# A new build-time order for a fused attention and expert kernel: counting DMA issues, the shared port of VectorE and GpSimd, idle PSUM banks and filler transposes

## The chip, the cores and the metric

The kernel runs on one core of one Trainium2 chip. The metric is the device time of one execution in microseconds, taken as the median of several executions. Each experiment was timed against the kernel before on the same chip in the same rounds. e1 to e4 ran on one chip and e5 to e12 on another. The kernel before took 1820.07 us on the first, and 1820.44 and 1820.51 us on the second, so a comparison of e1 with a later run can be off by about half a microsecond.

## The reference, cut to what matters

```python
# attention without softmax: 8 batches, 8 heads, 576 rows, 64 columns
kv  = einsum('bhsd,bhse->bhde', k, v)
out = einsum('bhsd,bhde->bhse', q, kv)
x   = out / sqrt(mean(out*out, -1) + 1e-6) * g_norm      # RMS norm
x   = x.transpose(0, 2, 1, 3).reshape(4608, 512)
# four experts, all of them applied to every row
p   = domain_probs / (domain_probs.sum(-1) + 1e-9)
for e in range(4):
    h    = maximum(x @ w1[e], 0)           # 512 -> 1024
    out += p[:, e:e+1] * (h @ w2[e])       # 1024 -> 512
```

Everything is float32. The 4608 rows are worked on as nine chunks of 512 rows, so there are 36 pairs of an up product (`w1`) and a down product (`w2`). In the attention, a "pair" is a pair of heads: a batch is worked on as four of them.

## The kernel before

Both products use a two-level scheme of block products in which seven products replace eight. It pays with additions: sums of blocks of `w1`, of `w2` and of `x` must exist before TensorE can multiply, and sums of results must be made after. VectorE and GpSimd make these sums; ScalarE copies and squares.

The order of all instructions is decided in Python when the kernel is built. Each operation has a key (how early it is wanted), an estimated cost on each engine that could do it, the buffers it reads and the buffers it writes. A simulation then runs through time and gives each free engine the ready operation with the smallest key:

```python
class Plan:
    CROSS, SAME = 0.3, 0.06
    REACH = {"PE": 0.7, "DVE": 0.9, "ACT": 0.9, "POOL": 0.9, "SP": 1.0}
    ...
    def layout(self, slots):
        ...
        while left:
            ...
            for eng in todo:                       # each engine that is free at time t
                for op in pending:                 # by key
                    when = ready(op, eng)          # inputs made, a buffer free
                    ...
                    if eng == "SP":                # a DMA issue
                        busy[eng] = t + op.cost[eng]
                        bus = max(bus, t + 1.5) + op.kb / 215.0
                        op.end = bus + 0.5
```

The parts that the change touches are the PSUM banks (the buffers into which TensorE writes its results; the kernel uses eight), the loads of the first attention batch, the weight sums, and the stores of the `x` sums:

```python
BANKS = {"ub": 4, "db": 2, "ab": 2}        # up products, down products, attention
SPC = {"SP": 0.08}                         # planned cost of one DMA issue
...
def combine(key, cost, out_, a, b, op, reads, writes):     # one sum, VectorE or GpSimd
    plan.add(key, cost, lambda eng: adder(eng).tensor_tensor(...), reads=reads, writes=writes)
...
def weights_1(e, key, step):
    ... # four loads of 512 KB, then the sums follow the loads at once
    form(key + 4 * step, 5, 21, 4, ALU.add)                # 1024 wide
    ...
    k2 = key + (8 + j) * step                              # 256 wide, four per outer block
...
def x_forms(c, key, step):                 # sums of x, then stores of 192 KB and 256 KB
    ...
attention(0, -2.0, 1.3, 0.1)               # keys: smaller is earlier
weights_1(0, -0.9, 0.02)
x_views = {0: x_forms(0, -0.2, 0.02)}
weights_2(0, 0.0, 0.02)
```

## Time and profile before

| quantity | before |
|---|---|
| time, median of 3 runs | 1820.47 us (1819.86 to 1820.76) |
| TensorE busy | 1784.6 us, 98% of the span of 1818.3 us |
| VectorE busy | 1126.2 us, 62% |
| GpSimd busy | 475.1 us, 26% |
| first up product starts | 41.76 us |
| first down product starts | 86.45 us |

TensorE is full but for the first 100 us. In a line of the windows below, the first two numbers are the stretch and its length; then come the busy microseconds (with the number of instructions) of TensorE, its weight loads, VectorE, ScalarE and GpSimd; then TensorE's granted clock, the share of the DMA engines and their GB/s. The prediction shows these rows up to 40 us. The next two of the kernel before are:

```profile
40.00:50.00 10.00, 9.98 (x63) 9.37 (x64) 9.33 (x17) 4.72 (x11) 9.84 (x17) 0.72 1.10 236
50.00:60.00 10.00, 6.88 (x70) 6.31 (x70) 9.90 (x15) 3.13 (x10) 6.50 (x5) 0.96 0.82 268
```

TensorE has gaps or a low clock here while VectorE is full (9.33 and 9.90 of 10). Below, "warm" means TensorE at full clock and "cold" at half of it. From the groups of the page come the two that make the large sums (line, engine, operation, shapes, count, then busy us and mean ns of one, then idle time before them and what ended it):

```profile
L276 DVE TENSOR_TENSOR big<-big,big 128x1024 f32<-128x1024 f32 x343 | 474.8, 1384 | 55.1 <-ACT big L680 33.2
...
L276 POOL TENSOR_TENSOR big<-big,big 128x1024 f32<-128x1024 f32 x85 | 209.0, 2462 | 1116.7 <-DVE big L276 976.1
```

VectorE's mean of 1384 ns is above the 1.22 us that one takes alone: some of them stood behind a GpSimd operation.

### The profile page before, as it was taken

The numbers are of one execution on the slowest core, as the hardware profiler recorded it, in microseconds if no ns is written. First come the engines' busy times: TensorE is split into PE (matmuls) and PEld (weight loads), VectorE is DVE, ScalarE is ACT, GpSimd is POOL, SyncE is SP. The second block draws the span as 40 slices with busy tenths as digits, with TensorE's granted clock in tenths as the row PEclk, the third lists the DMA queues.
The fourth block names the chain that finished last, engine by engine and source line by source line (L and its number), as shares of the span: only waits on it lengthen the run. The fifth ranks groups of instructions, "written<-read, shape, count | busy, mean of one in ns | idle before, by whom it ended". The sixth has DMA issues, their size and how long they took to land.

```text
span 1818.3 us, 32290 instructions
## 1 busy us (share of the span) xinstructions
PE 1784.6 (98%) x12496; PEld 1660.7 (91%) x12496; DVE 1126.2 (62%) x1841; ACT 608.4 (33%) x1345; POOL 475.1 (26%) x426
## 2 busy tenths in 40 slices
PE   5899999999999999999999999999999999999999
PEld 4889999999999999999999999999999999999997
DVE  6866665666676555555666555555566655556554
ACT  2544344443333333333333333333333333333331
POOL 4565554646364000000145000000036100000001
PEclk7999999999999999999999999999999999999999
DMA  9764444424433333334434333333434333343321
GB/s 231 179 167 141 128 139 126 135 95 139 132 109 119 117 114 115 114 113 134 136 130 152 118 118 118 118 118 121 147 127 163 117 115 117 118 118 116 115 74 35
DMA packets 192089, 228.96 MB, mean 126 GB/s; under 512 B 54464, under 2 KB 123328, under 8 KB 191936
## 3 DMA queue, kind: packets, MB, share of 16 engines
q1 hardware_dynamic: 191936, 226.89, 40.9%
q8 instruction: 99, 1.62, 0.4%
q14 instruction: 54, 0.44, 0.1%
HBM read 160.18 MB, written 66.65 MB: 125 GB/s over the span
## 4 chain that ended last, share of the span: by engine, by line
PE 94%; DVE 2%; SPq 2%; DMA 1%; issue 1%; POOL 0%; ACT 0%; DVEq 0%; ACTq 0%
PE ub L697 42%; PE db L831 29%; PE ab L831 18%; SPq L282 1%; PE ab L504 1%; PE ab L486 1%; DVE big L276 1%; PE ab L514 1%; PE ab L471 1%; DVE small L276 0%; DMA big<-in_moe_w_dram 0%; DMA small<-in_q_dram 0%; PE ab L553 0%; DVE big L718 0%; POOL big L276 0%
## 5 line engine op out<-in xcount | busy, mean ns | idle before, releaser
L831 PE MATMUL db<-big,big 128*128 128x256 f32 x2520 | 596.3, 380 | 1.7 <-DVE big L276 1.3
L697 PEld LDWEIGHTS ub<-small,big 128*128 128x128 f32 x3816 | 498.4, 192 | 23.4 <-issue 1.4
L697 PE MATMUL ub<-small,big 128*128 128x128 f32 x3816 | 513.5, 276 | 0.4 <-DVE big L718 0.4
L276 DVE TENSOR_TENSOR big<-big,big 128x1024 f32<-128x1024 f32 x343 | 474.8, 1384 | 55.1 <-ACT big L680 33.2
L831 PEld LDWEIGHTS db<-big,big 128*128 128x128 f32 x2520 | 455.2, 190 | 51.7 <-DVE big L276 1.5
L276 POOL TENSOR_TENSOR big<-big,big 128x1024 f32<-128x1024 f32 x85 | 209.0, 2462 | 1116.7 <-DVE big L276 976.1
L710 ACT ACTIVATE snap<-ub 128x256 f32<-128x256 f32 x756 | 285.5, 383 | 556.7 <-PE ub L697 500.8
L718 DVE TENSOR_TENSOR big<-ub,snap 128x256 f32<-128x256 f32 x756 | 307.0, 421 | 216.7 <-PE ub L697 163.1
L697 PE MATMUL ub<-small,w1y 128*128 128x128 f32 x2916 | 384.9, 276 | 2.2 <-DVE big L718 2.1
L697 PEld LDWEIGHTS ub<-small,w1y 128*128 128x128 f32 x2916 | 360.5, 192 | 7.9 <-DVE big L718 2.9
L831 PE MATMUL ab<-big,big 128*128 128x256 f32 x1512 | 357.4, 380 | 1.7 <-DVE small L788 1.7
L831 PEld LDWEIGHTS ab<-big,big 128*128 128x128 f32 x1512 | 273.2, 190 | 32.0 <-DVE small L788 2.1
L710 ACT ACTIVATE big<-ub 128x256 f32<-128x256 f32 x252 | 96.7, 384 | 414.6 <-PE ub L697 410.1
L788 DVE SCALAR_TENSOR_TENSOR small<-db,p_all,small 128x256 f32<-128x256 f32 x243 | 116.9, 481 | 139.8 <-PE db L831 139.2
L788 DVE SCALAR_TENSOR_TENSOR small<-ab,p_all,small 128x256 f32<-128x256 f32 x189 | 91.1, 482 | 177.3 <-PE ab L831 177.3
L680 ACT ACTIVATE big<-big 128x1024 f32<-128x1024 f32 x144 | 152.0, 1055 | 107.8 <-DVE big L276 104.8
L784 DVE TENSOR_SCALAR small<-db,p_all 128x256 f32<-128x256 f32 x72 | 34.6, 481 | 54.1 <-PE db L831 54.1
L425 POOL TENSOR_TENSOR rt<-ss,mhalf 128x8 f32<-128x8 f32 (+1 forms) x40 | 65.7, 1643 | 3.3
L421 POOL TENSOR_SCALAR ss<-ss 128x8 f32<-128x8 f32 (+1 forms) x40 | 15.6, 391 | 101.0 <-DVE ss L416 99.6
L416 DVE TENSOR_REDUCE ss<-small 128x8 f32<-128x512 f32 (+1 forms) x40 | 27.1, 678 | 22.3 <-ACT small L411 22.3
L504 PE MATMUL ab<-kvbd,small 128*128 128x128 f32 x256 | 38.3, 298 | 1.6 <-ACT kvbd L494 1.6
L432 DVE TENSOR_TENSOR small<-ab,rt 128x512 f32<-128x512 f32 (+1 forms) x40 | 27.4, 686 | 17.3 <-POOL rt L425 17.1
(63 smaller groups left out, 664.0 us busy)
## 6 DMA issues: line engine op xcount, KB each, us to landing
small<-x SPq DMA_DIRECT2D x189, 256.0 KB, 3.5
small<-x SPq DMA_DIRECT2D x189, 192.0 KB, 2.9
o<-small SPq DMA_DIRECT2D x108, 256.0 KB, 2.0
small<-o SPq DMA_DIRECT2D x108, 256.0 KB, 2.8
big<-in_moe_w_dram SPq DMA_DIRECT2D x32, 512.0 KB, 5.0
x<-small SPq DMA_DIRECT2D x63, 256.0 KB, 3.1
small<-in_q_dram SPq DMA_DIRECT2D x72, 128.0 KB, 3.9
kv<-in_k_dram SPq DMA_DIRECT2D x32, 288.0 KB, 3.5
```

The lines of the kernel that those rows point to most:

```text
L276: lambda eng: adder(eng).tensor_tensor(out=out_(), in0=a(), in1=b(), op=op),
L416: lambda eng: nc.vector.reduce_sum(out=ss.ap[0:n, :], in_=rows(sq), axis=AX.X),
L425: nc.gpsimd.tensor_tensor(out=rt.ap[0:n, :], in0=ss.ap[0:n, :], in1=mhalf[0:n, :], op=ALU.pow)
L432: lambda eng: nc.vector.tensor_tensor(out=rows(x), in0=rows(raw), in1=rt.ap[0:n, :].unsqueeze(2).to_broadcast([n, H, D]), op=ALU.mult,),
L504: nc.tensor.matmul(raw.ap[:, rs], lhsT=qT.ap[:, rs], rhs=kb.ap[:])
L680: lambda eng: nc.scalar.activation(out=b.ap[:], in_=b.ap[:], func=ACT.Relu),
L697: nc.tensor.matmul(ps.ap[:, u * P:(u + 1) * P], lhsT=w1f[e][m][mm][1]()[:, u * P:(u + 1) * P], rhs=views[m][mm][1](), start=(mm in (1, 2, ...
L710: lambda eng: nc.scalar.activation(out=where(), in_=ps.ap[:, 0:HN], func=ACT.Copy),
L718: lambda eng: nc.vector.tensor_tensor(out=block(whole, a, t), in0=src.ap[:, 0:HN], in1=add_.ap[:], op=ALU.add),
L784: nc.vector.tensor_scalar_mul(out=acc[i].ap[:, cols], in0=ps.ap[:, 0:HN], scalar1=prob)
L788: nc.vector.scalar_tensor_tensor(out=acc[i].ap[:, cols], in0=ps.ap[:, 0:HN], scalar=prob, in1=acc[i].ap[:, cols], op0=ALU.mult, op1=ALU.add,)
L831: nc.tensor.matmul(ps.ap[:, 0:HN], lhsT=four(h[m])[:, kt // 2, t, kt % 2, :], rhs=w2f[e][m].ap[:, kt * HN:(kt + 1) * HN], start=(m in (1, ...
```

## The change

Its intent is that the build-time order should be closer to what the chip does, and that the start should be shorter. It has six parts:

1. The order counts a DMA issue as 0.55 us in place of 0.08, and allows eight transfers in flight.
2. Two sums on VectorE and GpSimd never overlap in the plan (`port=True`).
3. Batch 0 of the attention uses the PSUM banks of the up and down products, which are idle then. TensorE gets filler transposes where the plan has it idle before the first up product.
4. All `q`, `k` and `v` of batch 0 are loaded first, two of the four pairs into big buffers. The up weights come next and the down weights later.
5. The weight sums have keys close to their use (`need`), so they come after the attention.
6. The `x` sums are made and stored in fewer and larger pieces.

Smaller parts came with these: the corner of a weight buffer that a sum writes over is tracked apart from the rest of the buffer, a block of an up product may start only after the last product of the block two before it, and only DMA issues must leave some buffers free.

```diff
-    CROSS, SAME = 0.3, 0.06
+    CROSS, SAME, LANES = 0.3, 0.06, 8
...
+            if eng == "SP":
+                when = max(when, lanes[0])
+            if op.port:
+                when = max(when, port)
             return when
...
+                if eng == "PE" and busy[eng] <= t and 1.6 <= t and front < idle_until:
+                    ...                      # two transposes of the identity into a free bank
-    BANKS = {"ub": 4, "db": 2, "ab": 2}
+    BANKS = {"u1": 2, "u2": 2, "db": 2, "ab": 2}
-    SPC = {"SP": 0.08}
+    SPC = {"SP": 0.55}
...
-            reads=reads, writes=writes,
+            reads=reads, writes=writes, port=True,
...
-        form(key + 4 * step, 5, 21, 4, ALU.add)
+        form(need + 0.25, 5, 21, 4, ALU.add)
...
-            kt, vt, qt = Buf("kv", f"k{n}"), Buf("kv", f"v{n}"), Buf("small", f"q{n}")
+            kind = "kv" if b or hp < 2 else "big"
+            kt, vt, qt = Buf(kind, f"k{n}"), Buf(kind, f"v{n}"), Buf("small", f"q{n}")
+            want = at(hp) - 0.25 if b else key - 1 + 0.1 * hp
...
-            bank = Buf("ab", f"kv{n}")
+            bank = Buf("ab" if b else "u1", f"kv{n}")
...                                          # x sums: one 256-wide and two 128-wide, not four 128-wide
...                                          # stores of 256 and 512 KB, not 192 and 256 KB
-    weights_1(0, -0.9, 0.02)
-    x_views = {0: x_forms(0, -0.2, 0.02)}
-    weights_2(0, 0.0, 0.02)
+    weights_1(0, -2.5, 0.02, -0.35)
+    x_views = {0: x_forms(0, -0.3)}
+    weights_2(0, 0.25, 0.02)
...
-                weights_1(e + 1, s + 0.0, 0.12)
+                weights_1(e + 1, s + 0.0, 0.12, s + 0.3)
...
-    order = plan.layout(slots)
+    order = plan.layout(slots, idle, ("u1", "u2", "db"), 0.0)
```

## The prediction

> **What bounds the kernel now.** I read the page first, then the table of windows, then the timelines of TensorE and VectorE over the first 160 us, then the chain of what ended last.
>
> ```profile
> PE 1784.6 (98%) x12496; PEld 1660.7 (91%) x12496; DVE 1126.2 (62%) x1841; ACT 608.4 (33%) x1345; POOL 475.1 (26%) x426
> ...
> PE   5899999999999999999999999999999999999999
> ```
>
> TensorE is busy all the time except in the first two slices of 45 us. The chain says how long a steady chunk takes; its rows have start, duration, engine, line:
>
> ```profile
> 198.06 1.78 PE ub L697 x16
> ...
> 257.86 1.78 PE ub L697 x16
> ...
> 688.75 3.12 PE ub L697 x28
> 734.81 3.12 PE ub L697 x28
> ```
>
> The same row of two neighbouring chunks is 46.06 us apart in the later experts and 59.80 us in the first one, where a batch of attention (59.80 - 46.06 = about 13.7 us) is mixed in. 36 chunks and 8 batches make 36 x 46.06 + 8 x 13.7 = 1768 us of TensorE work at full clock. The last product ends near 1813.8, and 4.5 us of merge and store follow. So 1813.8 - 1768 = 46 us are lost, and the windows show where (start:end, length, then busy time of each engine, clock):
>
> ```profile
> 0.00:10.00 10.00, 2.57 (x28) 2.11 (x29) 1.21 (x9) 1.88 (x2) 0.69 (x6) 1.00 0.69 153
> 10.00:20.00 10.00, 8.15 (x54) 6.81 (x52) 2.40 (x4) 3.78 (x9) 3.40 (x4) 1.00 1.13 317
> 20.00:30.00 10.00, 8.21 (x72) 7.09 (x72) 9.47 (x13) 2.93 (x8) 5.12 (x3) 0.58 1.18 246
> 30.00:40.00 10.00, 1.48 (x6) 0.79 (x6) 8.99 (x19) 1.28 (x2) 7.92 (x9) 0.50 0.80 207
> ...
> 600.00:900.00 300.00, 300.00 (x2003) 281.05 (x2002) 175.44 (x292) 93.05 (x206) 14.18 (x6) 1.00 0.39 123
> ```
>
> In 600 to 900 TensorE has no gap at all. Between 150 and 1800 the windows lack about 4 us of TensorE busy time in total, most of it where one expert's weights give way to the next. So some 42 of the 46 us are lost before 150 us. From 20 to 60 us VectorE is the full engine and TensorE waits for it:
>
> ```profile
> 28.28 2.08 PE L504 MATMUL ab<-kvbd,small 128*128 128x128 f32 x8 [0.55 <-ACT kvbd L494]
> 34.70 1.11 PE L514 MATMUL ab<-ident,small 128*128 128x128 f32 x4 [4.33 <-DVE small L432]
> 40.02 1.09 PE L514 MATMUL ab<-ident,small 128*128 128x128 f32 x4 [4.21 <-DVE small L432]
> 40.90 1.06 PE L471 MATMUL ab<-ident,small 128*128 128x128 f32 x4
> 41.76 1.91 PE L697 MATMUL ub<-big,big 128*128 128x128 f32 x8
> ...
> 108.03 1.05 PE L504 MATMUL ab<-kvbd,small 128*128 128x128 f32 x8
> ```
>
> The first up product starts at 41.76. By then 12.7 us of useful work are done (batch 0 of the attention, counted with the warm durations), so 29 us are lost. By the first down product at 86.45 the same count gives 42 us. The rest up to 157 us adds a little. The x8 group of L504 takes about 2.0 us early and 1.05 us later: TensorE runs at half clock then, though the page grants 1.00 in the first windows.
>
> **What the Trainium skill says.** (1) "TensorE: Matmul & The Clock Gate", Part 1, states that the array starts at half rate and reaches full rate after a busy window of about 3.4 us. The 2.08 against 1.05 us agrees with two rates. (2) The same page, Part 4, says that transposes do not count as TensorE busy time in the same way. This matters, since the change fills gaps with transposes; the trace before doesn't decide it. (3) "SBUF — State Buffer", section "SBUF: two separate sides", describes the port pair of VectorE and GpSimd as an exclusive lock, whose loser waits out the whole instruction. The trace agrees exactly:
>
> ```profile
> 20.36 4.84 POOL L276 TENSOR_TENSOR big<-big,big 128x1024 f32<-128x1024 f32 x2
> ...
> 21.04 1.95 DVE L276 TENSOR_TENSOR w1y<-big 128x256 f32<-128x256 f32 x1
> ...
> 22.91 3.37 DVE L276 TENSOR_TENSOR big<-big,big 128x1024 f32<-128x1024 f32 x1
> ```
>
> The two GpSimd operations take 2.42 us each and end at 22.78 and 25.20. VectorE's 256-wide operation, 0.42 us when alone, ends just after the first; its 1024-wide one, 1.22 us alone, ends about 1.1 us after the second. (4) "DMA: Bandwidth & Descriptors", section "Bandwidth", advises large transfers. Here the average DMA share after 150 us is 0.4, so the size of the stores can't matter much.
>
> **The change, part by part.** *x sums in larger pieces.* The order of issues shrinks from 961 to 745 rows. Bytes grow: per reload 7 x 512 KB instead of 7 x 448 KB, 0.45 MB more per 46 us, or 10 GB/s on about 120. No wait of TensorE after 150 us is put down to a DMA, so this is worth 0. Three additions per form become one 256-wide and two 128-wide (0.335 + 2 x 0.205 us by the spacing in VectorE's timeline, against 4 x 0.205): 7 x 0.08 = 0.5 us per chunk of an engine that has slack once the start is over.
>
> *Loads.* All q, k, v of batch 0 now come first, then expert 0's up weights, then batch 1, then the down weights. The four pairs are 3.33 MB. Before, 1.53 MB had moved by 10 us and 317 GB/s flowed after it, so the fourth pair lands near 10 + 1.8/0.317 = 15.7 us, and the up weights (2.1 MB) near 22. Before, the third pair's product started at 22.1 and the fourth's at 26.2. From the key-value product (8.52) to the last transposes (16.99) one pair took 8.5 us, so the fourth could reach its transposes near 24.2.
>
> *Fillers.* The changed order has 130 extra 128x128 transposes of the identity, 118 of them ahead of the first up product. A group of four takes about 0.44 us warm, so the 118 take 13.0 us warm and 26 us at half clock. They stand in TensorE's queue with the 12.3 us of real work: from 1.5 us on, 25.3 us of it, so the first up product can't start before about 27. With the first microseconds cold and a few waits on top I put it at 30. That is 11 to 12 us earlier than 41.76.
>
> *The VectorE order.* Attention now comes ahead of the weight sums on VectorE: the reductions of all four pairs stand before the first weight sum, so the 4.2 and 4.3 us waits go. But the weight sums are put off, not removed. Counting VectorE's rows in the new order with the durations above (1.13 us per 1024-wide, 0.6 per 512 and per reduction, 0.335 per 256, 0.2 per 128) gives about 41 us from the fourth pair's multiplication to the 21st sum of an up block (seven blocks' worth). The old order gives about 42 us for the like stretch and took 65 us for it (18.2 to 84). If the new order starts at 24.5 and loses 8 to 15 us to the port and to waits, in place of 24, it gets there at 74 to 81 us. TensorE will then have done 51.7 us of useful work by my count of its order, so 22 to 29 us are lost, against 42 to 43 before. That is 14 to 21 us won.
>
> *Rest.* Experts 2 to 4, the tail and the 4 us between experts stay: the products are the same, and in the new order two up blocks still run alternately with one down product in every five. The sum: 1820.5 less about 19 is **1801 us**.
>
> **The rivals.** *VectorE takes the place of the old wait.* If the fillers and earlier loads only bring TensorE sooner to a VectorE that is full anyway, the gain is 8 us or less, 1812. For: 9.47, 8.99, then 9.33 and 9.90 us busy out of each 10 between 20 and 60. Against: part of that was blocked time. *Cold fillers.* If transposes don't raise the clock, 118 of them cost 26 us, the first up product starts near 45, and the change is worth nothing or costs up to 8 us: 1820 to 1828. For: the skill's sentence. Against: real products stand among them and raised the clock before; the groups at 18.88 and 20.23 take 0.66 us, not 1.09. *New steady waits.* The up products get two pairs of banks instead of a pool of four, and port-exclusive planning may misplace sums. At 0.3 us a chunk this would eat 11 us: 1812. Against: about 3 us of other products stand between two writes of one bank, twice the copy and sum they wait for. *All goes well*: VectorE is never blocked and arrives at 68, then 1791.
>
> **Range and chances.** The best case loses 30 - 12.7 = 17 us before the first up product even with nothing after it, so more than 36 us cannot be won and faster by over 2% is nearly excluded. Slower by over 2% needs 1 us lost per chunk, which the even order speaks against. I take 1788 to 1815 with 1801 in the middle: faster 0.02, same 0.95, slower 0.03.
>
> **What would show it.** Right: first up product between 27 and 33; transposes of the last pair without 4 us waits; the first down product near 65 to 75; VectorE still above 9 of 10 between 30 and 60; GpSimd's and VectorE's 1024-wide operations no longer stretched; a steady chunk of 46.06 us; stalls between experts unchanged. Wrong: four transposes at 1.09 us up to 40 us (cold fillers); gaps of TensorE between 150 and 1800 over 10 us in total; a chunk over 46.3 us; or a first down product after 80.

## The result, and the profile after

| quantity | before | after |
|---|---|---|
| time, median (range) of 4 runs each | 1820.16 us (1819.74 to 1820.76) | 1806.80 us (1805.55 to 1807.96) |
| span of the profiled run | 1818.3 us | 1803.8 us |
| first up product starts | 41.76 us | 28.93 us |
| first down product starts | 86.45 us | 67.92 us |
| TensorE idle after 150 us (of the stretches to 1700 us) | 3.63 us | 1.25 us |

The ratio is 0.9926, with a 95% interval of 0.9909 to 0.9943: 13.4 us won. A ratio is the mean time of one kernel's runs over that of the other's in the same rounds, so it is not quite the ratio of the medians quoted. The idle time of a stretch is its length less TensorE's busy time.

These are the lines of the page after that answer to those of before:

```profile
PE 1788.7 (99%) x12626; PEld 1667.9 (92%) x12626; DVE 1010.0 (56%) x1757; ACT 614.3 (34%) x1345; POOL 582.0 (32%) x447
...
PE   8999999999999999999999999999999999999998
...
L304 POOL TENSOR_TENSOR big<-big,big 128x1024 f32<-128x1024 f32 x136 | 323.7, 2391 | 1005.9 <-DVE big L304 815.0
...
L304 DVE TENSOR_TENSOR big<-big,big 128x1024 f32<-128x1024 f32 x292 | 372.9, 1278 | 31.4 <-ACT big L728 13.3
```

VectorE lost 116 us of busy time. 102 us of it (474.8 less 372.9) are in the 1024-wide sums: GpSimd took 51 of them over, and the rest became shorter, 1278 ns in place of 1384. The windows after, in the same columns as above, are:

```profile
0.00:10.00 10.00, 8.06 (x68) 7.41 (x68) 1.21 (x9) 2.32 (x4) 0.69 (x6) 1.00 0.68 160
10.00:20.00 10.00, 9.38 (x117) 8.71 (x117) 3.21 (x5) 5.04 (x11) 3.70 (x4) 1.00 1.15 261
20.00:30.00 10.00, 10.00 (x108) 9.93 (x109) 6.66 (x12) 3.28 (x7) 6.92 (x7) 1.00 1.16 282
30.00:40.00 10.00, 9.07 (x112) 8.27 (x110) 7.81 (x17) 4.43 (x13) 6.00 (x7) 1.00 1.03 207
...
50.00:60.00 10.00, 6.57 (x71) 5.68 (x69) 9.54 (x14) 4.68 (x13) 8.93 (x8) 1.00 1.07 330
...
600.00:900.00 300.00, 300.00 (x2010) 281.25 (x2009) 165.18 (x282) 96.37 (x210) 42.20 (x18) 1.00 0.40 131
```

The hole from 30 to 40 us is gone (9.07 where it was 1.48), and the clock no longer drops to a half. Much of the busy time of the first three rows is filler, though. Between 50 and 60 us TensorE still waits, and VectorE (9.54) and GpSimd (8.93) are full together. From 70 to 150 us TensorE has no gap.

In the timeline of TensorE after, columns are start, duration, engine, line, operation, shapes and count, and in brackets an idle time before it with what ended it. L927 are the fillers, L521 the key-value product, L549 the transposes of the finished attention rows, L745 the up product, L882 the down product:

```profile
1.34 4.10 PE L927 MATMUL u<-ident 128*128 128x128 f32 x18 [1.34 <-POOL ident masks.py:199]
...
8.20 0.92 PE L521 MATMUL u<-kv,kv 96*64 96x64 f32 x24
...
25.00 3.66 PE L927 MATMUL u<-ident 128*128 128x128 f32 x32
28.50 0.60 PE L549 MATMUL u<-ident,small 128*128 128x128 f32 x4
28.93 1.06 PE L745 MATMUL u<-big,big 128*128 128x128 f32 x8
...
67.92 1.89 PE L882 MATMUL db<-big,big 128*128 128x256 f32 x8
```

The last transposes of the batch stand at 28.50 without a wait, where before they started at 40.02 behind a wait of 4.21 us. The chain of what ended last shows two neighbouring chunks after:

```profile
643.61 1.78 PE u L745 x16
...
689.67 1.78 PE u L745 x16
```

They are 46.06 us apart, exactly as before. So all of the gain comes from the start and, with about 2.4 us, from the places where one expert's weights give way to the next.

### The profile page after: what moved, and what is told of

Read it like the earlier page. It is cut to its first block, busy times and chain, and to the rows that moved or that the text cites. A ratio compares the mean times of both kernels' runs of the same rounds, so it can differ in the third digit from the quotient of the medians.

```text
span 1803.8 us, 31919 instructions
## 1 busy us (share of the span) xinstructions
PE 1788.7 (99%) x12626; PEld 1667.9 (92%) x12626; DVE 1010.0 (56%) x1757; ACT 614.3 (34%) x1345; POOL 582.0 (32%) x447
## 4 chain that ended last, share of the span: by engine, by line
PE 97%; DVE 1%; POOL 1%; SPq 1%; DMA 0%; ACT 0%; issue 0%; POOLq 0%; DVEq 0%; ACTq 0%
PE u L745 44%; PE db L882 30%; PE ab L882 18%; PE ab L539 1%; PE ab L521 1%; PE ab L549 1%; PE ab L506 1%; SPq L310 1%; PE ab L588 0%; DMA big<-in_v_dram 0%; PE u L927 0%; POOL big L304 0%; DVE big L304 0%; POOL rt L458 0%; PE ab L603 0%
## 5 line engine op out<-in xcount | busy, mean ns | idle before, releaser
L304 POOL TENSOR_TENSOR big<-big,big 128x1024 f32<-128x1024 f32 x136 | 323.7, 2391 | 1005.9 <-DVE big L304 815.0
L882 PE MATMUL db<-big,big 128*128 128x256 f32 x2520 | 594.6, 379 | 0.7 <-POOL big L304 0.7
L882 PEld LDWEIGHTS db<-big,big 128*128 128x128 f32 x2520 | 455.7, 190 | 50.8 <-POOL big L304 1.1
L745 PEld LDWEIGHTS u<-xf,big 128*128 128x128 f32 x3600 | 470.2, 192 | 20.9 <-issue 0.9
L761 ACT ACTIVATE snap<-u 128x256 f32<-128x256 f32 x756 | 290.1, 384 | 585.3 <-PE u L745 497.2
L745 PE MATMUL u<-xf,big 128*128 128x128 f32 x3600 | 486.1, 276 | 0.1
L769 DVE TENSOR_TENSOR big<-u,snap 128x256 f32<-128x256 f32 x756 | 314.8, 422 | 240.0 <-PE u L745 124.0
L304 DVE TENSOR_TENSOR big<-big,big 128x1024 f32<-128x1024 f32 x292 | 372.9, 1278 | 31.4 <-ACT big L728 13.3
L745 PE MATMUL u<-xf,w1y 128*128 128x128 f32 x2700 | 357.1, 275 | 0.7 <-DVE big L769 0.6
L882 PE MATMUL ab<-big,big 128*128 128x256 f32 x1512 | 357.4, 379 | 0.0
L745 PEld LDWEIGHTS u<-xf,w1y 128*128 128x128 f32 x2700 | 334.6, 192 | 5.8 <-DVE big L769 1.0
L882 PEld LDWEIGHTS ab<-big,big 128*128 128x128 f32 x1512 | 273.3, 190 | 29.8
L761 ACT ACTIVATE big<-u 128x256 f32<-128x256 f32 x252 | 96.8, 384 | 413.3 <-PE u L745 410.9
L304 POOL TENSOR_TENSOR xf<-xf 128x128 f32<-128x128 f32 (+1 forms) x74 | 47.8, 656 | 17.6 <-DVE xf L304 15.2
L745 PE MATMUL u<-small,big 128*128 128x128 f32 x216 | 33.6, 280 | 0.6 <-ACT snap L761 0.5
```

The lines of the kernel that those rows point to most:

```text
L304: lambda eng: adder(eng).tensor_tensor(out=out_(), in0=a(), in1=b(), op=op),
L745: nc.tensor.matmul(ps.ap[:, u * P:(u + 1) * P], lhsT=w1f[e][m][mm][1]()[:, u * P:(u + 1) * P], rhs=views[m][mm][1](), start=(mm in (1, 2, ...
L761: lambda eng: nc.scalar.activation(out=where(), in_=ps.ap[:, 0:HN], func=ACT.Copy),
L769: lambda eng: nc.vector.tensor_tensor(out=block(whole, a, t), in0=src.ap[:, 0:HN], in1=add_.ap[:], op=ALU.add),
L882: nc.tensor.matmul(ps.ap[:, 0:HN], lhsT=four(h[m])[:, kt // 2, t, kt % 2, :], rhs=w2f[e][m].ap[:, kt * HN:(kt + 1) * HN], start=(m in (1, ...
```

## The experiments

Twelve kernels ran, all with correct results. The texts name some theories by letters. A: the attention stands behind the weight sums on VectorE, and the new sequence frees it. B: the fillers, which keep the clock up and are worth the gain. D: the port rule of the order. E: idle banks and early loads let the attention of batch 0 finish earlier. F: the sum of VectorE's and GpSimd's work before about 60 us sets the time, not the first up product.

| run | built on | median (range), us | ratio to before, 95% interval | first up / first down, us |
|---|---|---|---|---|
| after | | 1806.80 (1805.55 to 1807.96) | 0.9926 [0.9909, 0.9943] | 28.93 / 67.92 |
| e1_nofill | after | 1805.54 (1804.43 to 1806.23) | 0.9917 [0.9900, 0.9934] | 28.89 / 67.79 |
| e2_before_fill | before | 1820.81 (1818.20 to 1822.05) | 1.0001 [0.9986, 1.0016] | 42.34 / 84.55 |
| e3_before_w1late | before | 1857.82 (1857.43 to 1858.16) | 1.0206 [1.0191, 1.0221] | 44.68 / 89.70 |
| e4_before_kv_w1late | e3 | 1853.87 (1852.57 to 1858.62) | 1.0189 [1.0174, 1.0205] | 39.94 / 92.18 |
| e5_abonly | e1 | 1816.96 (1813.12 to 1817.18) | 0.9976 [0.9961, 0.9991] | 35.70 / 79.36 |
| e6_loadsold | e1 | 1821.85 (1819.58 to 1822.59) | 1.0006 [0.9991, 1.0021] | 39.95 / 81.83 |
| e7_noport | e1 | 1834.68 (1833.27 to 1836.34) | 1.0079 [1.0064, 1.0094] | 29.28 / 64.49 |
| e8_oldx | e1 | 1807.58 (1806.35 to 1809.20) | 0.9929 [0.9912, 0.9946] | 28.06 / 64.42 |
| e9_w1first | e1 | 1807.04 (1806.11 to 1808.64) | 0.9926 [0.9911, 0.9941] | 37.35 / 78.19 |
| e10_dve6 | e1 | 1812.00 (1811.77 to 1812.42) | 0.9953 [0.9936, 0.9970] | 27.84 / 73.24 |
| e11_nodma | e1 | 1810.67 (1810.26 to 1812.22) | 0.9947 [0.9932, 0.9962] | 28.09 / 70.64 |
| e12_best | e1 | 1803.32 (1802.71 to 1803.64) | 0.9904 [0.9890, 0.9919] | 27.87 / 61.91 |

One caution holds for all of them. A planner makes a new order for each edit, so a run tells what the edit does together with the order that the planner then finds.

### e1_nofill: the changed kernel without fillers

```diff
-    order = plan.layout(slots, idle, ("u1", "u2", "db"), 0.0)
+    order = plan.layout(slots, idle, ("u1", "u2", "db"), -1e9)
```

> The changed kernel without the filler transposes of the identity; the order of the other work is nearly the same up to the first up products. Theory A (the gain comes from the attention no longer standing behind weight sums and weight loads): TensorE is cold in the attention of batch 0, so the last pair's own key-value products, attend and transposes take about 2.2 us longer in its chain (1.55 for 0.92, 2.08 for 1.06, 1.1 for 0.6), the 1.2 us by which fillers held up the last transposes is won, and the first up products are cold for some 3 to 4 us: first up product near 30, 1808 to 1811 us, 1 to 4 us over the changed kernel. Theory B (the gain is the warm clock that the fillers keep): most of the 13.4 us is lost, 1815 us or more. Theory C (fillers only stand in the way): 1803 to 1806.

The time was 1805.54 us, no slower than with fillers. From TensorE's timeline of this run:

```profile
8.28 1.55 PE L521 MATMUL u<-kv,kv 96*64 96x64 f32 x24 [1.19 <-DMA kv<-in_v_dram]
...
28.01 1.08 PE L549 MATMUL u<-ident,small 128*128 128x128 f32 x4 [2.95 <-DVE small L465]
28.89 1.91 PE L745 MATMUL u<-big,big 128*128 128x128 f32 x8
```

The fillers do raise the clock: the same key-value product took 0.92 us at 8.20 with them and 1.55 us at 8.28 without. The first up product takes 1.06 us with them and 1.91 us without. But it starts at the same moment, because it waits for VectorE and not for TensorE's own work: the last transposes were idle for 2.95 us and could start at 28.01. With fillers the multiplication before them ended at 27.27, and the transposes stood behind a filler group until 28.50. Faster products at this place only wait longer. Theory B fell.

### e2_before_fill: the kernel before with the fillers alone

```diff
-    order = plan.layout(slots)
+    order = plan.layout(slots, idle, ("ub", "db"), 0.0)     # and the filler code of the change
```

> The kernel before with the fillers alone (110 groups, two transposes each). Theory A: VectorE still does weight sums ahead of the attention, so the first up product stays near 40 (38 to 43) and the time at 1814 to 1822; the warm clock can win the 2 to 4 us that early up products now spend cold. Theory B: first up product near 33 and 1812 us or less.

Its 1820.81 us are those of the kernel before. Fillers keep TensorE's clock at 1.00 from 20 to 50 us here too (before: 0.58, 0.50 and 0.72), and the first up product is still at 42.34. This is the second result against B.

### e3_before_w1late: the kernel before with late weight sums alone

```diff
-        form(key + 4 * step, 5, 21, 4, ALU.add)
+        form(need + 0.25, 5, 21, 4, ALU.add)        # the other forms and the 256-wide sums likewise
-    weights_1(0, -0.9, 0.02)
+    weights_1(0, -0.9, 0.02, -0.35)
-                weights_1(e + 1, s + 0.0, 0.12)
+                weights_1(e + 1, s + 0.0, 0.12, s + 0.3)
```

> The kernel before, with one part of the change: the sums of the up weights stand behind the attention in the build-time order (loads, storage, cost model, banks as before). Theory A: the waits of 4.3 and 4.2 us for VectorE's multiplication go; keys and values of the third and fourth pair still land at 22 and 26, so the first up product is near 35 to 38 and the time 1812 to 1817. Theory B (fillers) and theory D (planning with the shared port and DMA issues makes the gain): 1818 to 1822, since neither is in it.

It was 37 us slower than before, clear of the noise (by the 2% rule this is "unclear", as for e4, since both intervals contain 1.02). The waits of TensorE (engine and line waiting, for what, us in total, times, longest) and one of its windows show where a good part went:

```profile
PE ub L697 <- DVE big L718: 23.0, 14, 5.1
```

```profile
500.00:600.00 100.00, 91.55 (x594) 84.86 (x593) 71.22 (x106) 27.70 (x61) 49.42 (x31) 0.98 0.35 115
```

After 150 us this kernel is idle for 23.0 us where the kernel before was for 3.6: 8.45 us from 500 to 600, and 6.8 in each of the stretches with a later expert boundary. That is over half of the loss. The rest is at the start, where the up products come at 44.68 and run at half clock from 20 to 60 us. The same keys are in the changed kernel, and there these boundaries cost 1.25 us in all. So late sums alone do harm. What makes them harmless there was not told apart. It is not the port rule alone: e7 has late sums without that rule, and its two later boundaries cost only 1.3 us each (idle from 900 to 1300 and from 1300 to 1700), though its first one costs 14.1.

### e4_before_kv_w1late: late sums and early loads together

The edit is e3 and, in `attention`, the `kind` and `want` lines of the change. A version with early loads alone could not be built: the planner came to a state in which no operation could start.

> As the one before, and also the third and fourth pair's keys and values in buffers of their own, loaded ahead of the weights. Theory A: first up product near 30 to 33 at cold clock, and 1806 to 1811, so nearly the whole gain with neither fillers nor a new cost model nor new storage. Theories B and D: 1814 or more.

Its 1853.87 us are 34 us worse than before. By the medians they are 4 us better than e3, but the ranges overlap. The first up product came at 39.94, 1.8 us earlier than before. This settled theory A as far as it goes: the sequence of sums and loads isn't enough. The timeline showed the key-value products of the third and fourth pair at 19.52 and 25.37, held by the two attention banks.

### e5_abonly: the changed kernel with only the attention's own banks in batch 0

```diff
-            bank = Buf("ab" if b else "u1", f"kv{n}")
+            bank = Buf("ab", f"kv{n}")        # "raw" and "xT" likewise; no fillers
```

> The changed kernel without fillers (1805.5 us), with one part undone: the attention of batch 0 has only the two ab banks of PSUM again, in place of the idle banks of the up and down products as well. Theory E (the banks and the early loads let the four pairs of batch 0 follow each other every 4 us): pairs three and four are held by the two banks, key-value products near 19.5 and 25 as in the kernel before with late sums, first up product at 33 to 36 in place of 28.9, and 1810 to 1813. If the banks don't matter: 1805 to 1807 and first up product at 29.

Taking the idle banks away costs about 11 us (0.9976 against 0.9917). From its timeline of TensorE:

```profile
25.41 1.55 PE L521 MATMUL ab<-big,big 96*64 96x64 f32 x24 [0.75 <-ACT small L511]
...
33.97 1.09 PE L549 MATMUL ab<-ident,small 128*128 128x128 f32 x4 [3.54 <-DVE small L465]
```

The fourth pair's product is at 25.41 where e1 has it at 20.96, with the same loads: two banks hold two results at a time. TensorE ran at half clock from 20 to 40 us (0.50 and 0.54 granted).

### e6_loadsold: the changed kernel with the old places of the loads

```diff
-            want = at(hp) - 0.25 if b else key - 1 + 0.1 * hp
+            want = at(hp) - 0.25                # and all pairs in kv buffers, no fillers
-    weights_1(0, -2.5, 0.02, -0.35)
+    weights_1(0, -0.9, 0.02, -0.35)
```

> The changed kernel without fillers, with the other part undone: keys and values of pairs three and four in the four kv buffers again, requested at their old place, with the up weights among them. Theory E: these keys and values land near 20 and 24, first up product at 32 to 35 and 1808 to 1812. If loads are hidden: 1805 to 1807.

This loses the whole gain: 1821.85 us. From its timeline of TensorE:

```profile
26.07 1.55 PE L521 MATMUL u<-kv,kv 96*64 96x64 f32 x24 [0.70 <-DMA kv<-in_v_dram]
...
36.57 1.11 PE L549 MATMUL u<-ident,small 128*128 128x128 f32 x4 [4.19 <-DVE small L465]
```

The fourth pair waits for its `v` until 26.07, as in the kernel before (26.18). VectorE, which has the weight sums put behind the attention, is then idle: 1.97 and 6.11 us busy in the windows of 20 to 30 and 30 to 40. Without the early loads nothing of the gain is left; without the idle banks some 3 us of it are (e5, 0.9976). So nearly all of the gain needs both. This supports E.

### e7_noport: the changed kernel without the port rule

```diff
-            if op.port:
-                when = max(when, port)          # and no fillers
```

> The changed kernel without fillers, and without the rule that plans VectorE's and GpSimd's two-input operations one at a time. Theory D (the port rule is what keeps VectorE from being blocked in the stretch from 30 to 70 us): GpSimd operations run into VectorE's again, the 1024-wide mean on VectorE rises from 1278 back to about 1380 ns, the first down product comes 5 to 10 us later and the time is 1810 to 1815. If the start is set by the attention alone: 1804 to 1807.

This was the costliest part to lose: 1834.68 us, 29 us above e1 and 14 above the kernel before. The group of large sums and one window of this run are:

```profile
L302 DVE TENSOR_TENSOR big<-big,big 128x1024 f32<-128x1024 f32 x341 | 474.0, 1390 | 57.2 <-ACT big L726 38.2
```

```profile
500.00:600.00 100.00, 85.88 (x541) 77.91 (x540) 61.94 (x92) 24.51 (x55) 47.51 (x32) 0.97 0.31 106
```

Without the rule VectorE makes 341 of the large sums at a mean of 1390 ns, which are the numbers of the kernel before (343 and 1384). The rule is thus also what gave GpSimd the 51 sums. The timelines of VectorE and GpSimd show one collision:

```profile
34.11 2.44 DVE L302 TENSOR_TENSOR small<-big,small 128x128 f32<-128x128 f32 x1
```

```profile
33.60 2.80 POOL L302 TENSOR_TENSOR big<-big,big 128x1024 f32<-128x1024 f32 x1
```

A VectorE sum of 128 elements, 0.28 us elsewhere, ends at 36.55, just after GpSimd's at 36.40. The 29 us, however, are not near the start alone. TensorE is idle for 14.1 us from 500 to 600 where e1 is for 1.25, and its first down product is even earlier, at 64.49. How much of it is time on the port and how much a worse order stays open, since the rule can't be removed without a new plan.

### e8_oldx: the changed kernel with the old sums and stores of x

The edit puts back four 128-wide sums per form, the stores of 192 and 256 KB, and the old buffers for them. It has no fillers.

> The changed kernel without fillers, with the x sums formed by four 128-wide additions and stored in the old pieces of 64 to 256 KB. By the prediction, storage is worth nothing: 1804.5 to 1807. A rival: the three-instruction form saves VectorE and GpSimd time in the full stretch, and the fewer issues unblock the queue that loads the next keys and values: then 1808 to 1812.

1807.58 us, 2 us above e1 with overlapping intervals (0.9912 to 0.9946 against 0.9900 to 0.9934). TensorE was idle for 4.2 us after 150 us in place of 1.25. The larger pieces are worth some 2 us at most, and the study can't tell it from nothing.

### e9_w1first: up weights loaded and summed before the attention

```diff
-    weights_1(0, -2.5, 0.02, -0.35)
+    weights_1(0, -4, 0.02, -1.6)               # no fillers
```

> The changed kernel without fillers (1805.5 us), but with the up weights loaded ahead of all q, k, v, and their sums planned ahead of the attention. The attention gets its data 8 us later, so the first up product comes at 37 to 41 in place of 28.9. Theory A (the start of the up products sets the time): 1813 to 1817. Theory F (VectorE's and GpSimd's sums up to some 60 us set it, and the early gap of VectorE from 8 to 24 us is now used for them): 1800 to 1807 in spite of the late first product, with TensorE's gaps between 40 and 70 us nearly gone.

This is the run that told the two remaining theories apart. The first up product came at 37.35, 8.5 us later than in e1. The first down product was 10 us later, at 78.19. The time was 1807.04, within 1.5 us of e1's. Two of its windows:

```profile
40.00:50.00 10.00, 10.00 (x87) 9.52 (x87) 5.94 (x13) 4.43 (x11) 4.93 (x5) 0.81 0.99 282
50.00:60.00 10.00, 8.63 (x71) 7.80 (x70) 9.05 (x14) 5.33 (x15) 8.28 (x7) 1.00 0.91 298
```

TensorE, started late, is then full at 40 to 50 us (e1: 8.99) and at 8.63 from 50 to 60 (e1: 6.83), because VectorE had done its sums while it would otherwise wait for the attention. What VectorE did in its early gap shows in the window from 10 to 20 us, where it is busy for 8.29 us (e1: 2.57):

```profile
10.00:20.00 10.00, 5.08 (x40) 4.58 (x40) 8.29 (x15) 1.63 (x4) 0.00 (x0) 1.00 1.18 221
```

Neither the start of the first up product nor that of the first down product sets the time by itself; e8 says the same from the other side, with a first down product at 64.42 and no gain. This supports F.

### e10_dve6: more work for VectorE at 50 us

```diff
-            nc.vector.reduce_sum(out=tot[:], in_=p_all[:], axis=AX.X)
+            for _ in range(21):
+                nc.vector.reduce_sum(out=tot[:], in_=p_all[:], axis=AX.X)    # no fillers
```

> The changed kernel without fillers, the order of everything the same, but 20 more reductions of the probabilities (about 0.27 us each, one input, some 5.5 us together) on VectorE near 50 us. Theory F (VectorE is the full engine of that stretch): the time grows by 4 to 5.5 us, to 1809.5 to 1811. If attention, loads or TensorE set the end of the stretch: 0 to 2 us, 1805.5 to 1807.5.

The timeline of VectorE and a window of this run:

```profile
49.37 7.04 DVE L333 TENSOR_REDUCE tot<-p_all 128x36 f32<-128x144 f32 x21
```

```profile
60.00:70.00 10.00, 8.01 (x42) 6.61 (x39) 7.66 (x12) 3.08 (x7) 7.42 (x7) 0.50 0.41 121
```

The same place in e1:

```profile
49.00 0.29 DVE L332 TENSOR_REDUCE tot<-p_all 128x36 f32<-128x144 f32 x1
49.33 1.30 DVE L333 TENSOR_SCALAR tot<-tot 128x36 f32<-128x36 f32 x1
...
51.90 0.41 DVE L769 TENSOR_TENSOR big<-u,snap 128x256 f32<-128x256 f32 x1
```

From the first reduction to the next up-block sum VectorE needs 7.92 us here (49.37 to 57.29) and 2.90 us in e1 (49.00 to 51.90), so 5.0 us were added. The 20 reductions took 6.75 us, but two operations after them met no GpSimd sum here and took 1.7 us less than in e1 (the TENSOR_SCALAR 0.18 us in place of 1.30, where it ended 0.05 us after a GpSimd sum). The time rose by 6.5 us, from 1805.54 to 1812.00. There is no slack on VectorE at this point, and TensorE's clock, which fell to 0.50 from 60 to 70 us, adds to the wait.

### e11_nodma: the changed kernel without counting DMA issues

```diff
-            if eng == "SP":
-                when = max(when, lanes[0])
-    SPC = {"SP": 0.55}
+    SPC = {"SP": 0.08}                          # the load of probs 0.3 us, not 1.8; no fillers
```

> The changed kernel without fillers, planned with the old cheap DMA issue (0.08 us) and without the limit of eight in flight. The first 17 load instructions stand in the same order, after them batch 1's keys and values stand behind the down weights and five q loads. So I expect the first up product still at 29, a later attention of batch 1, and 1806 to 1812; 1804 to 1806.5 if batch 1's loads are early enough anyway.

1810.67 us, some 5 us above e1, with intervals that just touch (0.9932 to 0.9962 against 0.9900 to 0.9934). First up product 28.09, first down product 70.64: the loss is between them, where TensorE is busy for 7.25 and 6.81 us in the windows from 30 to 50 (e1: 8.71 and 8.99).

### e12_best: a version with better keys

If VectorE's work before 60 us is the bound, the stretch from 12 to 24 us, in which it mostly waits for the attention, should be filled. This version lets the weight sums start earlier, and puts the down weights and the stores at other places:

```diff
-    weights_1(0, -2.5, 0.02, -0.35)
-    x_views = {0: x_forms(0, -0.3)}
-    weights_2(0, 0.25, 0.02)
+    weights_1(0, -2.5, 0.02, -0.9)
+    x_views = {0: x_forms(0, -0.4)}
+    weights_2(0, 0.4, 0.02)
-                key + 0.9, SPC,                             # stores of the x sums
+                key + 0.7, SPC,
-                attention(c + 1, s - 0.1, 0.8, s + 0.5)
+                attention(c + 1, s - 0.1, 0.9, s + 0.5)     # no fillers
```

> A version meant to beat the changed one: no fillers, the sums of the up weights planned ahead of the last pairs' attention so that VectorE uses its gaps before 25 us, down weights a little later, batch 1's attention spread wider, x stores earlier. Theory F: 1800 to 1804. If the first up product alone matters (it stays at 28 to 30): 1804 to 1807.

1803.32 us, within what theory F had said (1800 to 1804) and the best: 17 us below the kernel before, and 3.5 us below the changed kernel by the medians. VectorE was busy for 9.23 us from 20 to 30 (e1: 6.76), and the first down product came at 61.91. The interval (0.9890 to 0.9919) overlaps that of the changed kernel in its other rounds slightly, though no run of the one reached a run of the other (at most 1803.64 against at least 1805.55). Several keys were moved at once, so this supports F without isolating it.

## Why the prediction was right or wrong

The time of 1806.80 us was inside the range of 1788 to 1815 and inside "within 2%", 5.8 us above the 1801 named. By its own steps:

**Storage worth 0: right as far as it can be told.** e8 gives 2 us or less, not separable from 0, and no wait for a DMA after 150 us came or went with it.

**First up product at 30: right in the number (28.93), with half of the cause.** The prediction let TensorE's queue decide it: 13.0 us of fillers and 12.3 us of work from 1.5 us on. In the changed kernel the fillers did end last: the last transposes could have started at 27.27 and stood behind a group of fillers until 28.50. But without the queue of fillers nothing is won: e1 has none and starts at 28.89. What holds it there, and would have held the changed kernel at nearly the same time, is the chain of the fourth pair. Its loads landed later than the 15.7 us estimated: the product waited for `v` and started at 19.93. Then square, reduction (23.70), the GpSimd power, the multiplication (26.58 to 27.27) and the transposes follow one another. The idle PSUM banks and the load order shorten this chain (e5, e6). That the two bounds lay within about a microsecond of each other was luck for the prediction. From VectorE's timeline after, the end of that chain, the first weight sum between, and the sum at 84.10 that the term after next speaks of:

```profile
23.70 0.69 DVE L449 TENSOR_REDUCE ss<-small 128x8 f32<-128x512 f32 x1 [0.74 <-ACT small L444]
24.30 0.42 DVE L304 TENSOR_TENSOR w1y<-big 128x256 f32<-128x256 f32 x1
...
26.58 0.69 DVE L465 TENSOR_TENSOR small<-db,rt 128x512 f32<-128x512 f32 x1 [0.45 <-POOL rt L458]
...
84.10 0.42 DVE L769 TENSOR_TENSOR big<-u,snap 128x256 f32<-128x256 f32 x1
```

**No wait of 4 us at the last transposes, first down product at 65 to 75, a steady chunk of 46.06 us: right** (none, 67.92 and 46.06). Of its other signs, VectorE above 9 of 10 from 30 to 60 us held only from 40 on (7.81, 9.18 and 9.54), and the 1024-wide sums came near their unstretched length without reaching it (a mean of 1278 ns on VectorE against 1.22 us alone; 2391 ns on GpSimd, 2462 before).

**Stalls between experts unchanged: wrong by 2.4 us in our favour.** They fell from 3.63 to 1.25 us.

**The VectorE order worth 14 to 21 us: this term of the sum failed.** The up product of a chunk is made of seven blocks with three VectorE sums each; the prediction let the last of the 21 end at 74 to 81 us with 22 to 29 us lost. Its first weight sum stood at 24.30, as assumed (24.5). But the 21st sum was at 84.10, hardly earlier than in the kernel before (86.00; the prediction's 84 is the 20th sum there, at 83.94). With TensorE's last product ending near 1799.2, the total lost by the prediction's own count is 1799.2 - 1768 = 31 us, in place of 46. Of these, 16.6 are gone at the first up product (28.93 less 12.3) against 29 before. So 12.4 us of the gain stand at that point, and the further 7 of its 19 did not come (19 is itself above the middle of its 14 to 21). Since TensorE has no gap from 70 to 150 us and 1.25 us of idle time after, some 30 us were lost by the mark (an estimate), just outside the 22 to 29. Two readings of the traces say why. Until about 60 us VectorE and GpSimd are full together (9.54 and 8.93 from 50 to 60) and TensorE waits for them; e10 shows that work added there is paid in full. From about 62 us on it is VectorE that waits for TensorE, in eight of the sums up to 86 us, for about 8 us in all, and TensorE is full from 70 us. The mark chosen, VectorE's 21st sum, thus lay beyond the point where VectorE stops being the bound, and its date said how much TensorE had already lost, not how fast VectorE was.

**That the 12.8 us at the first up product equal the gain of 13.4 us is a coincidence.** e9 starts the first up product 8.5 us later and loses 1.5 us by the medians.

The rival "VectorE takes the place of the old wait" (1812) had the right mechanism and was too pessimistic by 5 us. "Cold fillers" fell: after the first 18 the fillers were warm (32 of them in 3.66 us at 25.00). "New steady waits" didn't appear.

Where the time shows up can be added up from the windows of the kernel before and of e1, which has no fillers to count as work. "Cold" is busy time times one less the granted clock, between 20 and 100 us:

| TensorE, us | before | e1 | won |
|---|---|---|---|
| idle, 0 to 20 | 9.3 | 9.0 | 0.3 |
| idle, 20 to 40 | 10.3 | 5.8 | 4.5 |
| idle, 40 to 70 | 3.1 | 4.9 | -1.8 |
| idle, 70 to 150 | 2.7 | 0.2 | 2.5 |
| cold, 20 to 100 | 8.6 | 4.0 | 4.6 |
| idle, 150 to 1700 | 3.6 | 1.25 | 2.4 |
| sum | 37.6 | 25.1 | 12.5 |

The spans of the two differ by 13.8 us (1818.3 less 1804.5), so 1.3 us are not placed; some products between 10 and 20 us are shorter in e1 while the clock column says 1.00 for both. The table says where, not why. Filling the idle and cold time of 0 to 40 us with transposes changed both columns of the changed kernel and not its time. What decides, as far as e9, e10 and e12 show it, are the sums that VectorE and GpSimd have to make by about 60 us: how early they may begin (loads and banks), and how few of them stand behind one another on the port.

The losses by removal (about 11 us for the banks, 16 for the loads, 29 for the port rule, 5 for the DMA issues) add up to far more than the 13.4 us won, so they are not shares of the gain: each was removed while the others stayed. The late weight sums were never undone alone in the changed kernel; e12, which moves them earlier along with other keys, is 2.2 us faster than e1.

Two things stay open. The 29 us of the port rule are not split between waits on the port and a worse order; TensorE's idle and cold time account for some 25 of them (19.9 idle, 4.8 cold), 13 at one expert boundary. And it is open why late weight sums cost 20 us at the boundaries in e3 and next to nothing in the changed kernel.

## What to carry to other kernels

Ask of a wait that is to be removed which engine has to do how much work before the next stretch that is full, and date the end of that work, not the start of the first instruction that becomes possible. Keeping TensorE warm with fillers was worth nothing here, where it waited for another engine (e1, e2). The static order gained from knowing which two engines can't run at once (e7), and parts of such a change (early loads, idle banks, late sums) can each be useless or harmful alone, so they should be tested by removal from the whole as well as by addition to the old.

## What the Trainium skill lacked or had wrong

- "TensorE: Matmul & The Clock Gate", Part 4: PE-mode transpose, says that the full clock doesn't engage for transposes. Here 18 float32 transposes alone from 1.34 us took 4.10 us (228 ns each), a later group of 32 took 3.66 us (114 ns each), and the next key-value product after only transposes took 0.92 us against 1.55 us without them. Float32 transposes did raise the clock.
- "SBUF — State Buffer", SBUF: two separate sides, describes the shared pair as an exclusive lock, and the traces agree: a VectorE sum of 0.28 us took 2.44 us and ended 0.15 us after GpSimd's. What it lacks is what planning around the lock is worth: 1390 ns against 1275 ns for a mean 1024-wide VectorE sum, and 29 us of the kernel's time (e7 against e1, the new order included).
- The lock was met even in a plan that forbids it: in e1 a GpSimd sum that a DMA had delayed by 0.64 us coincided with a 256-wide VectorE sum, which took 2.56 us in place of 0.42 us. No page speaks of fixed orders and their dates.
